# Expert slots of four, three, two and one units in a fused attention and expert kernel

## The chip, the cores and the metric

The kernel runs on one core of a Trainium2 chip. Its time is the device time of one execution in microseconds. The median of 3 runs before the change is 802.62 us (801.01 to 803.15).

## The reference

Two stages follow each other. The first is attention by feature maps: for each of 8 batches and 8 heads with 576 tokens of 64 numbers

```
phi(x) = [exp(p), exp(-p)],  p = x @ w_phi - max|x @ w_phi|      (128 features, so 256)
kv = phi(k)^T v,   z = sum over tokens of phi(k)
x = phi(q) kv / (phi(q) z + 1e-6)                                (8 heads side by side: 512 numbers)
```

The second is a layer of 8 experts over the 4608 tokens. A token takes the expert with the largest logit of `x @ w_gate`, or, if it is not the first of its batch and a local gate is at least 0.5, the expert of the token before it. Then

```
h = relu(x @ w1[e])          (512 -> 1024)
out = p[e] * (h @ w2[e])     (1024 -> 512),  p = softmax(logits)
```

So the list of tokens of each expert is known only once attention is done, and it depends on the data.

## The kernel before

**Attention** (`step`, L400) is a loop of 72 steps of two chunks of 128 tokens: projection, exponentials, sums over keys, output, and the gate's logits. The 4608 tokens come in four quarters (`bp` 0 to 3). When a quarter's logits are there, `gate` (L452) runs beside the following steps as a generator, a few small DVE operations a step: it finds each token's expert, its rank in the expert's list and its probability, and scatters the pairs (token, probability) to `lst` in DRAM with nine indirect DMAs on POOL (L571). The gate of the last quarter can only run behind attention.

**Units and slots.** A unit is 128 tokens of one expert's list. A slot is a number of units of one expert: its weights are loaded once, eight pieces of 512 KB (four of `w1`, four of `w2`, `load`, L848). A piece lands in a staging tile `wraw`, ACT rounds it to `whi` (L876), and DVE makes the residue `wlo` (L877). Each product is three matmuls, hi by hi, hi by lo and lo by hi (`three`, L941). Before the change there are quads (four units, done as two groups of two), pairs and singles; and "duals", slots that do a half unit of each of two experts at once, straight in f32 (L956).

**Layer 1** (`layer1`, L958) of a group of two units holds the weights in the array and moves the tokens: 8 blocks of hidden features by 4 blocks of inputs by 3 products, 96 matmuls with 256 moving columns. Two blocks of features share one PSUM bank (`psl`, two banks); ACT evacuates it with a relu to `hh` (L978) and DVE makes the residue `hl` (L979). A single holds the tokens and moves the weights (48 matmuls of 256 columns), which leaves the hidden layer the wrong way round: it is transposed on TensorE by 8 transposes (`turn`, L995). **Layer 2** (`layer2`, L1010) holds 128 tokens of the hidden layer and moves 512 columns of weights: 24 matmuls a unit. The result is scaled on DVE (L1030) and scattered to the output by an indirect DMA on POOL (L1033).

**Tokens** are fetched a unit at a time by an indirect DMA (L904) and turned by four transposes (L929) into `xhi` and `xlo`. `slots` (L1042) runs a list of slots; it turns the next slot's tokens within the current one (`between`, `rest`) and loads the coming slots' weights each time that a weight buffer comes free (`used`, `spare`). There are 13 weight buffers (`WE`, `WR`, `WL`: 8 + 4 + 1), of which 12 exist during the early slots.

**Early slots and the plan.** Three early pairs fill the time in which the last gate and the plan of the rest are made. `plan_early` (L666) places two of them once half of the tokens are known and one more at three quarters; their lists are fetched and turned, and the first slot's weights are loaded, still beside attention. In the first early slot's layer 1 the list `soon` runs a step of the last gate after certain blocks (`go` is one step, `rest` is all that is left, which ends with the nine scatters). `more` runs one part of `plan_main` (L727): the first part counts the units of each expert, cuts them level by level (quads, pairs, singles), makes each unit's row in the list and issues the fetch of the lists (`lr`, L633); the second turns the fetched lists on TensorE (L646) to `tok` and `prob`. The first `more` stands in the second unit of the first early slot's layer 2, the second in that of the second slot. After the early slots the memory of attention is given back (`open_rest`), and with it comes the second set of weight staging tiles.

The number of slots of each size is fixed: 3 quads, 7 pairs, 4 singles and 2 duals always run. Units that find no place run one at a time in a loop behind a condition (`guarded`, L1069); the last slot's output is written behind that condition (`held`). The order of the main slots is written out in `moe` (L1104): the quads first, then the pairs, with a single or a dual after every one or two of them. TensorE's order is the program's, but for small moves of the compiler's own planner.

## Time and profile before

| | before |
|---|---|
| median of 3 runs | 802.62 us (801.01 to 803.15) |
| the profiled execution | 799.24 us |
| its span | 797.3 us |
| granted TensorE clock, mean | 0.991 |
| TensorE busy | 771.4 us, 97% of the span |
| VectorE (DVE) busy | 511.8 us, 64% |
| ScalarE (ACT) busy | 401.6 us, 50% |
| GpSimd (POOL) busy | 159.8 us, 20% |
| HBM | 128.21 MB read, 22.06 MB written |
| attention | up to 318.2 us |
| three early slots | 318.2 to 406.3 us |
| sixteen main slots | 406.3 to 791.3 us |

All times in a row of the profile are microseconds from the span's start, a mean is in ns. A group's line has the source line, the engine, the operation, what it writes and reads with shapes, the count, then its busy time, the mean of one, and the idle time of the engine ahead of it with what ended it. TensorE's matmuls overlap in the pipeline, so that their shown durations are longer than the distance from one start to the next. "issue" is time in which an engine waited for nothing that the profile shows. Of the rows by stretch, the columns are the stretch, its length, the busy time and count of PE, PEld (weight loads), DVE, ACT and POOL, the granted TensorE clock, the DMA engines' mean busy share, and GB/s.

### The profile page before, as it was taken

What the parts mean: (1) busy time and instruction counts of PE and PEld (TensorE: products, weight loads), DVE (VectorE), ACT (ScalarE), POOL (GpSimd) and SP (SyncE); (2) the same over time, 40 slices, a digit from 0 to 9 for tenths busy, and PEclk for the clock granted to TensorE, in tenths of its full rate; (3) what the DMA queues carried; (4) which work ended last, traced back from release to release, by engine and by line L of the source; (5) the groups of instructions that cost most, each with busy time, mean ns of one, the idle gap of its engine ahead of it and who ended that gap; (6) DMA issues with size and microseconds to landing.
All of it is one profiled execution on the core that took longest, in us unless ns stands there. A gap on an engine that the chain in (4) does not pass through costs nothing.

```text
span 797.3 us, 23203 instructions
## 1 busy us (share of the span) xinstructions
PE 771.4 (97%) x9674; PEld 678.8 (85%) x9674; DVE 511.8 (64%) x939; ACT 401.6 (50%) x708; POOL 159.8 (20%) x174
## 2 busy tenths in 40 slices
PE   7999999999999999969999999999999999999997
PEld 6999989988888878958899898598999999499996
DVE  5787798789878876956654223742965941759641
ACT  4666666666687655523543022631844721748431
POOL 0200002200375132152331201211222211111010
PEclk9999999999999999988999999999999999999999
DMA  7755545444687521716942575842867749968500
GB/s 205 228 154 136 132 133 147 127 132 123 204 250 230 170 62 42 219 37 219 401 166 85 195 270 220 293 133 97 312 218 232 291 151 403 388 230 292 199 34 29
DMA packets 75595, 151.29 MB, mean 190 GB/s; under 512 B 8524, under 2 KB 48652, under 8 KB 75446
## 3 DMA queue, kind: packets, MB, share of 16 engines
q1 hardware_dynamic: 67280, 127.27, 49.4%
q0 software_dynamic: 8032, 22.45, 7.8%
q8 instruction: 77, 1.26, 0.6%
q14 instruction: 30, 0.25, 0.1%
q10 hardware_dynamic: 176, 0.07, 0.0%
HBM read 128.21 MB, written 22.06 MB: 188 GB/s over the span
## 4 chain that ended last, share of the span: by engine, by line
PE 85%; DVE 7%; issue 3%; DMA 3%; ACT 2%; POOLq 0%; SPq 0%; another core or an unknown queue 0%; POOL 0%; DVEq 0%; ACTq 0%
PE l L943 15%; PE l L944 15%; PE l L945 15%; PE kvp L269 9%; PE nm L328 9%; PE pj L227 8%; PE qt L247 4%; PE l L956 4%; DMA wraw<-in_w1h 2%; PE tr L929 2%; DVE m L230 2%; DVE sb L232 1%; PE nm L307 1%; PE nm L295 1%; ACT kp L236 1%
## 5 line engine op out<-in xcount | busy, mean ns | idle before, releaser
L876 ACT CAST whi<-wraw 128x1024 fp32r<-128x1024 f32 x136 | 142.2, 1047 | 160.2 <-PE l L945 61.9
L877 DVE TENSOR_TENSOR wlo<-wraw,whi 128x1024 fp32r<-128x1024 f32 x128 | 156.3, 1222 | 76.3 <-ACT whi L876 69.6
L943 PE MATMUL l<-xhi,whi 128*128 128x256 f32 x512 | 146.9, 287 | 2.4 <-issue 1.4
L944 PE MATMUL l<-xlo,whi 128*128 128x256 f32 x512 | 144.4, 282 | 1.3 <-issue 1.3
L945 PE MATMUL l<-xhi,wlo 128*128 128x256 f32 x512 | 144.5, 282 | 0.9 <-issue 0.9
L943 PE MATMUL l<-whi,hh 128*128 128x512 f32 x288 | 114.8, 398 | 4.7 <-DVE p_rim L621 4.1
L230 DVE TENSOR_REDUCE m<-pj 128x8 f32<-128x1024 f32 x72 | 87.8, 1219 | 46.4 <-PE pj L227 44.2
L945 PE MATMUL l<-whi,hl 128*128 128x512 f32 x288 | 113.3, 393 | 0.6 <-DVE hl L979 0.6
L944 PE MATMUL l<-wlo,hh 128*128 128x512 f32 x288 | 113.0, 392 | 0.0
L250 ACT ACTIVATE qp<-qt 128x512 f32<-128x512 f32 x144 | 84.9, 604 | 55.4 <-PE qt L247 55.1
L236 ACT ACTIVATE kp<-sb 128x512 f32<-128x512 f32 x144 | 82.8, 622 | 51.5 <-DVE sb L232 42.3
L943 PEld LDWEIGHTS l<-xhi,whi 128*128 128x128 f32 x512 | 97.6, 191 | 4.5 <-issue 2.0
L945 PEld LDWEIGHTS l<-xhi,wlo 128*128 128x128 f32 x512 | 97.6, 191 | 2.2 <-issue 2.1
L944 PEld LDWEIGHTS l<-xlo,whi 128*128 128x128 f32 x512 | 97.6, 191 | 1.4 <-issue 0.9
L232 DVE TENSOR_TENSOR sb<-pj,m 128x1024 f32<-128x1024 f32 x72 | 88.1, 1224 | 4.1
L328 PE MATMUL nm<-kvs,qp 128*64 128x74 f32 x2304 | 88.0, 228 | 1.8 <-issue 1.4
L227 PE MATMUL pj<-first,kq 64*128 64x128 f32 x1152 | 85.7, 289 | 4.1 <-DMA kq<-in_kqT 4.1
L1033 POOL DMA_INDIRECT out<-y,p_tokm x31 | 39.2, 1264 | 245.0 <-DVE y L1030 232.0
L328 PEld LDWEIGHTS nm<-kvs,qp 128*64 128x64 f32 x2304 | 79.8, 136 | 3.5 <-issue 2.6
L227 PEld LDWEIGHTS pj<-first,kq 64*128 64x128 f32 x1152 | 71.8, 191 | 9.4 <-issue 4.1
L269 PE MATMUL kvp<-v,kp 128*64 128x65 f32 x2048 | 76.7, 224 | 0.1
L978 ACT ACTIVATE hh<-l 128x512 fp32r<-128x512 f32 x64 | 38.0, 594 | 69.7 <-PE l L945 60.3
(230 smaller groups left out, 1059.3 us busy)
## 6 DMA issues: line engine op xcount, KB each, us to landing
wraw<-in_w1h SPq DMA_DIRECT2D x68, 512.0 KB
wraw<-in_w2h SPq DMA_DIRECT2D x68, 512.0 KB
kq<-in_kqT SPq DMA_DIRECT2D x47, 384.0 KB
v<-in_va SPq DMA_DIRECT2D x48, 195.0 KB
xs<-xo SPq DMA_DIRECT2D x48, 128.0 KB
whi<-in_w1h SPq DMA_DIRECT2D x8, 512.0 KB
wlo<-in_w1h SPq DMA_DIRECT2D x8, 512.0 KB
whi<-in_w2h SPq DMA_DIRECT2D x8, 512.0 KB
```

The costliest lines, as they stand in the source:

```text
L227: self.last_pe = self.pe.matmul(t[:, h, i % 2, j, :], kq[r, j, s], self.w2[r], start=True, stop=True)
L230: dve.tensor_reduce(m, f, AX.X, ALU.max, apply_absolute_value=True)
L232: self.last_dve = dve.tensor_sub(sb.rearrange("p h c j f -> p (h c j) f"), f, m.unsqueeze(2).broadcast_to([128, 8, 128]))
L236: self.last_act = act.activation(kp[:, :, :, sg, :].rearrange("p c h f -> p h c f"), sb[:, :, :, 0], AF.Exp, scale=1.0 - 2 * sg)
L250: self.act.activation(qp[:, sg], t, AF.Exp, scale=1.0 - 2 * sg)
L269: self.pe.matmul(self.kvp[r, sg, h], self.ch[i]["kp"][:, h, sg, r], self.v(i, b)[:, h], start=first and n < 2, stop=last and n >= 6)
L328: self.pe.matmul(e["t"][r, c - c0, h, :], self.ch[i]["qp"][:, sg, h, q0 + r.start:q0 + r.stop], kvs[:, sg, h, :], start=sg == 0, stop=sg == 1)
L876: self.act.copy(hi, raw)
L877: (low or self.dve).tensor_sub(lo, raw, hi.bitcast(F32))
L943: mm(o, ah, bh, start=first, stop=False)
L944: mm(o, ah, bl, start=False, stop=False)
L945: self.last_pe = mm(o, al, bh, start=False, stop=last)
```

## The change

A slot now has four, three, two or one units, and all its tokens are the moving columns of layer 1 at once: 512, 384 or 256 columns for each held block of weights, 96 matmuls in each case. With three or four units, one block of features fills a tile of PSUM; with two, two blocks do. Quads are no longer two groups. Singles keep the old form (`layer1_one`), which duals use too.

There are 2 early slots of three units, both placed at half of the tokens, in place of 3 of two; 4 quads, 4 threes, 1 pair and 2 duals in the main list, and no single outside the guarded loop, which now may run up to 14. The main order is quad and three in turn, then the pair, with the duals third and seventh. `plan_main` has one more level (units by three, by a multiplication and a shift), and a new generator `table` works out the constants of it on DVE during seven attention steps. All of the next slot's tokens are turned within layer 2 of the current slot, or within layer 1 of a single or a dual. Steps of the gate and of the plan now stand after every six matmuls or block: four gate steps in slot 0's layer 1, the first part of the plan in the third unit of slot 0's layer 2, the second in slot 1's layer 1. The tiles of `x` and of the hidden layer exist once, the second set of weight staging has two tiles for three, and one weight buffer moves from the pool that is there early to the one that comes later (8 + 3 + 2).

```diff
-WE, WR, WL = 8, 4, 1
+WE, WR, WL = 8, 3, 2
...
-HALFWAY, EARLY, QUADS, PAIRS, SINGS, GUARD, DUALS, GUARD_D = 2, 3, 3, 7, 10, 6, 4, 2
-NUE = 2 * EARLY
+EARLY, QUADS, TRIPS, PAIRS, ONES, GUARD, DUALS, GUARD_D = 2, 4, 4, 1, 14, 14, 4, 2
+SINGS = 3 * TRIPS + ONES
+SIZES = ((4, QUADS), (3, TRIPS), (2, PAIRS), (1, ONES))
+FIRST = {4: 0, 2: 4 * QUADS, 3: 4 * QUADS + 2 * PAIRS, 1: 4 * QUADS + 2 * PAIRS + 3 * TRIPS}
+NUE = 3 * EARLY
...
+                    if p == FILL + 4:
+                        self.background.append(self.table())
...
-            self.slots(self.eslots, soon=[no, self.fetched_last, go, no, go, no, go, rest], later=[[no, no, more]] * 2)
+            self.slots(self.eslots, soon=[[no, no, no, go, no, no, go, no, no, go, rest], [no, no, no, no, more]],
+                       later=[[no, no, more]])
...
+    def table(self):
+        dve = self.dve
+        t = self.const.tile([NU, 16], F32, name="table")
+        c = [t[:, i:i + 1] for i in range(16)]
+        u, (v, size, rest, q, two, one, notq) = self.tokid[0:NU, 0:1], [self.slotc[:, i:i + 1] for i in range(7)]
...
+        def by_three(o, x, n):
+            dve.tensor_scalar(o, x, 3.0, None, ALU.is_ge)
+            for k in range(2, n):
+                dve.scalar_tensor_tensor(o, x, 3.0 * k, o, ALU.is_ge, ALU.add)
+        yield STEP
+        by_three(eth, u, EARLY)
+        dve.scalar_tensor_tensor(erest, eth, -3.0, u, ALU.mult, ALU.add)
+        yield STEP
+        dve.tensor_scalar(c[11], u, 2.0, None, ALU.mult)
+        dve.tensor_scalar(c[12], u, 2.0, 1.0, ALU.mult, ALU.add)
...
+        self.eslot, self.eparts, self.duo = eth, erest, t[:, 11:13]
+        self.mslot = cq, sz, half
+        self.kinds, self.pasts = (q, three, two, real), (notq, past, real)
...
-        if bp in (1, 2):
-            self.background.append(self.plan_early(bp))
+        if bp == 1:
+            self.background.append(self.plan_early())
...
+        f = self.floats(self.thirds(self.units_so_far(0, 7, "e"), "e"), "fe")
...
+        slots = [dict(ei=[ei[3 * i:3 * i + 1]], u=3 * i, n=3, name=f"e{i}", rows=2 * TB) for i in range(EARLY)]
         self.eslots += slots
...
+        f = self.fetch(es, k, NUE, "e", WAIT)
...
+        yield from self.early_chores(slots, got())
...
+        for i, (n, cap) in enumerate(SIZES):
+            if n == 3:
+                fi = self.thirds(r, "3")
+            elif n == 1:
+                fi = r
+            else:
+                fi = self.psm([NU, E], f"fi{n}", I32)
+                dve.tensor_scalar(fi, r, n.bit_length() - 1, None, ALU.logical_shift_right)
+            f = self.floats(fi, f"f{n}")
+            ins = self.prefix(f, f"i{n}")
+            incl, cnt = mix(ins, incl, kind[i], f"im{n}"), mix(f, cnt, kind[i], f"cm{n}")
+            if n > 1:
+                pl = self.placed(f, ins, cap, f"pl{n}")
+                dve.tensor_scalar_mul(pl, pl, float(n))
+                nr = self.psm([NU, E], f"r{n}", I32)
+                dve.tensor_sub(nr, r, pl)
+                r = nr
+                bef = mix(pl, bef, past[i], f"bef{n}")
+        i1 = ins
...
-        self.mxt = self.mkpool(root, "moe_x2", 2, "right")
+        self.mxt = self.mkpool(root, "moe_x2", 1, "right")
...
-            dst = [rp.tile([128, 1024], F32, name="wraw", bufs=3)]
+            dst = [rp.tile([128, 1024], F32, name="wraw", bufs=3 if rp is self.mxg else 2)]
...
+                p = self.mxt if n > 1 else self.ml1
+                s["x"] = [p.tile([128, 4, n * 128], F32R, name=x + "1" * (n == 1)) for x in ("xhi", "xlo")]
...
-    def layer1(self, s, gi, between, soon=()):
-        pe, act, dve = self.pe, self.act, self.dve
-        xh, xl = s["x"][gi]
-        w, last = s["w"], gi == len(s["n"]) - 1
-        hp = self.ml1 if gi else self.mx2
-        hh = hp.tile([128, 8, 256], F32R, name="hh", bufs=1)
-        hl = hp.tile([128, 8, 256], F32R, name="hl", bufs=1)
-        s.setdefault("h", []).append((hh, hl))
-        if s["n"][gi] == 2:
-            for f2 in range(4):
-                t = self.psl.tile([128, 2, 256], F32, name="l1")
-                wh, wl = w[f2]
-                for j in (0, 1):
-                    for d in range(4):
-                        c = slice(d * 256 + j * 128, d * 256 + j * 128 + 128)
-                        self.three(t[:, j, :], wh[:, c], wl[:, c], xh[:, d, :], xl[:, d, :], d == 0, d == 3)
-                    if soon:
-                        soon[2 * f2 + j]()
-                hc = slice(2 * f2, 2 * f2 + 2)
-                act.activation(hh[:, hc, :], t, AF.Relu)
-                dve.scalar_tensor_tensor(hl[:, hc, :], t, 0.0, hh[:, hc, :].bitcast(F32), ALU.max, ALU.subtract)
-                if between:
-                    between.pop(0)()
-                if last:
-                    self.used(1)
-                else:
-                    self.spare()
-            return []
...
+    def hidden(self, n):
+        return [self.mx2.tile([128, 8, n * 128], F32R, name=x, bufs=1) for x in ("hh", "hl")]
+    def layer1(self, s, between):
+        act, dve = self.act, self.dve
+        (xh, xl), w, n = s["x"], s["w"], s["n"]
+        hh, hl = s["h"] = self.hidden(n)
+        def pause():
+            if between:
+                between.pop(0)()
+        per = 2 if n == 2 else 1
+        for f0 in range(0, 8, per):
+            t = self.psl.tile([128, per, n * 128], F32, name="l1")
+            for j in range(per):
+                f = f0 + j
+                wh, wl = w[f // 2]
+                for d in range(4):
+                    c = slice(d * 256 + f % 2 * 128, d * 256 + f % 2 * 128 + 128)
+                    self.three(t[:, j, :], wh[:, c], wl[:, c], xh[:, d, :], xl[:, d, :], d == 0, d == 3)
+                    if d % 2 and (d, j) != (3, per - 1):
+                        pause()
+            hc = slice(f0, f0 + per)
+            act.activation(hh[:, hc, :], t, AF.Relu)
+            dve.scalar_tensor_tensor(hl[:, hc, :], t, 0.0, hh[:, hc, :].bitcast(F32), ALU.max, ALU.subtract)
+            pause()
+            if (f0 + per) % 2 == 0:
+                self.used(1)
+    def layer1_one(self, s, between):
+        pe, act = self.pe, self.act
+        xh, xl = s["x"]
+        hh, hl = s["h"] = self.hidden(1)
+        hs = self.ml1.tile([128, 1024], F32, name="hs", bufs=1)
...
-            if between and q in (0, 2):
+            if between:
...
     def slots(self, order, held=None, soon=(), later=()):
         first = order[0]
-        for g in range(len(first["n"])):
-            for f in self.tokens(first, g):
-                f()
+        for f in self.tokens(first):
+            f()
         self.held = len(first.get("w", ()))
         self.coming = list(order)
         for i, s in enumerate(order):
             while len(s.get("w", ())) < 8:
                 self.spare()
             new = order[i + 1] if i + 1 < len(order) else None
-            last = len(s["n"]) - 1
-            for gi in range(last):
-                self.layer1(s, gi, [])
-            between = self.tokens(new, 0, bool(soon) and i == 0) if new else []
-            rest = self.layer1(s, last, between, () if i else soon)
+            between = self.tokens(new, bool(soon) and i == 0) if new else []
+            if s["n"] > 1:
+                self.layer1(s, list(soon[i]) if i < len(soon) else [])
+                rest = between
+            else:
+                rest = self.layer1_one(s, between) + between
             if i < len(later):
-                rest = list(later[i])
-            for f in between:
+                rest = rest + list(later[i])
+            self.layer2(s, rest, None if new else held)
+            for f in rest:
                 f()
-            for gi in range(last + 1):
-                self.layer2(s, gi, rest, None if new else held)
-            if new and len(new["n"]) == 2:
-                for f in self.tokens(new, 1):
-                    f()
             s.clear()
...
-        few = self.ss[:SINGS - GUARD]
+        big = [x for i in range(max(QUADS, TRIPS)) for n in (4, 3) for x in self.by_size[n][i:i + 1]]
+        order = big + self.by_size[2] + self.by_size[1][:ONES - GUARD]
         for i, x in enumerate(self.ds[:DUALS - GUARD_D]):
-            few.insert(3 * i, x)
-        rest = self.qs + self.ps_
-        order = []
-        per = len(rest) / len(few)
-        for i, x in enumerate(few):
-            order += rest[round(i * per):round((i + 1) * per)] + [x]
+            order.insert(2 + 4 * i, x)
```

166 lines of the change are left out of this document (64 added, 102 removed).

## The prediction

> **What bounds the kernel now.** I read the page's share of engines, then the busy time by stage, then the chain of waits, then single instructions in order of time.
>
> ```profile
> PE 771.4 (97%) x9674; PEld 678.8 (85%) x9674; DVE 511.8 (64%) x939; ACT 401.6 (50%) x708; POOL 159.8 (20%) x174
> ```
>
> Busy time by stage (columns: stretch, us, busy and count of PE, PEld, DVE, ACT, POOL, granted clock, DMA share, GB/s). The stretches are attention, the three early slots, the main slots, the end:
>
> ```profile
> 4.00:318.20 314.20, 307.72 (x6678) 276.16 (x6679) 250.03 (x542) 200.12 (x429) 60.54 (x80) 1.00 0.54 156
> 318.20:406.30 88.10, 78.31 (x486) 68.30 (x484) 61.55 (x167) 39.38 (x48) 29.16 (x27) 0.94 0.64 218
> 406.30:791.30 385.00, 384.99 (x2515) 334.30 (x2513) 199.38 (x229) 160.64 (x230) 67.95 (x56) 1.00 0.60 214
> 791.30:797.30 6.00, 0.36 (x2) 0.00 (x0) 0.75 (x1) 0.00 (x0) 0.98 (x1) 0.70 0.11 44
> ```
>
> TensorE sets the main stage: idle for 0.01 us of 385, with ACT and DVE about half empty. Fewer casts or weight loads buy nothing there; only a shorter TensorE stream does. The early stage is the one with idle time. Its busy time overlaps (matmuls are pipelined), so what a matmul really takes is read from starts. TensorE's instructions, first and last of a run of 120 at 256 columns and of 96 at 512:
>
> ```profile
> 516.44 0.36 PE L943 MATMUL l<-xhi,whi 128*128 128x256 f32 x1
> 530.48 0.28 PE L945 MATMUL l<-xhi,wlo 128*128 128x256 f32 x1
> ...
> 429.93 0.40 PE L943 MATMUL l<-whi,hh 128*128 128x512 f32 x1
> 451.60 0.40 PE L945 MATMUL l<-whi,hl 128*128 128x512 f32 x1
> ```
>
> (530.48 - 516.44) / 119 = 0.1180 us at 256 columns and 21.67 / 95 = 0.2281 us at 512. The shown 0.28 and 0.40 are not costs. So doubling the columns nearly doubles the time: only 2 x 0.1180 - 0.2281 = 0.008 us of a matmul is fixed. No row has 384 columns. In proportion it is 0.171 by the one row and 0.177 by the other; at worst it is as slow as 512. I take the middle of the rows, 0.1731, since both lie on nearly one line through zero.
>
> **The main stage, part by part.** Before, layer 1 there is 13 groups of two units (three quads of two groups, seven pairs) of 96 matmuls and four singles of 48, all at 256 columns: (1248 + 192) x 0.1180 = 169.9 us. After, it is 384 at 512, 384 at 384 and 96 at 256: 87.6 + 66.5 + 11.3 = 165.4. That is **-4.5**. Layer 2 stays: the same 30 units of 24 matmuls at 512.
>
> The singles go, and with them their turning of the hidden layer. One single slot:
>
> ```profile
> 561.60 0.28 PE L943 MATMUL l<-whi,xhi 128*128 128x256 f32 x1
> 565.06 0.28 PE L945 MATMUL l<-whi,xlo 128*128 128x256 f32 x1
> 565.17 0.38 PE L995 MATMUL tr<-first,hs 128*128 128x128 f32 x2
> 565.31 0.36 PE L943 MATMUL l<-whi,xhi 128*128 128x256 f32 x1
> 566.45 0.60 PE L929 MATMUL tr<-first,xg 128*128 128x128 f32 x4
> 566.80 0.36 PE L943 MATMUL l<-whi,xhi 128*128 128x256 f32 x1
> 574.54 0.28 PE L943 MATMUL l<-xhi,whi 128*128 128x256 f32 x1
> ```
>
> Two transposes cost 0.14 us, four times per single, four singles: **-2.2**. A set of four token transposes costs 0.35; there is one per unit in both kernels. Sixteen main slots become eleven; the single took 12.94 us to the next slot's start, 0.5 more than 48 x 0.1180 + 24 x 0.2281 + 4 x 0.14 + 2 x 0.35, so a switch costs up to 0.5, at least 0; I take 0.4: **-2.0**. The 40 expert weights saved (five slots) are 20 MB of loads, 40 casts and 40 differences on engines with room here: 0, covered by TensorE's own work. The sum is **-8.7**, with bounds -5 (0.177, switches free) and -10 (0.171, 0.5 a switch). At 0.2281, which the rows speak against, it would be +12, and +11 more in the early stage.
>
> The plan must fit. The counts that the reference's routing gives for its inputs leave (3 4 6 3 3 3 4 4) units per expert after two early threes; four quads, four threes and one pair take exactly these 30, so the guarded loop does not run.
>
> **The early stage.** Its TensorE work is before 3 x (96 x 0.1180 + 48 x 0.2281) = 66.8, six token sets 2.1 and some 2 for the gate's small matmuls: 71 of 88.1 us, so 17 are lost. After, 2 x (96 x 0.1731 + 72 x 0.2281) = 66.1, eight sets 2.8 and 2: again 71. What changes is the loss. TensorE, DVE and POOL in order of time, then TensorE's clock:
>
> ```profile
> 348.50 0.96 POOL L571 DMA_INDIRECT lst<-pr,ri  x1 [0.30 <-issue]
> 349.64 0.28 PE L944 MATMUL l<-xlo,whi 128*128 128x256 f32 x1 [0.83 <-issue]
> 351.07 0.17 DVE L584 TENSOR_TENSOR_SCAN p_i<-p_one,p_f 36x8 f32<-36x8 f32 x1 [1.11 <-DVE p_ohh L792]
> 354.03 0.60 ACT L978 ACTIVATE hh<-l 128x512 fp32r<-128x512 f32 x1 [9.41 <-DVE p_kh L795]
> 359.21 0.13 DVE L621 TENSOR_SCALAR p_rim<-p_rowm 36x1 int32<-36x1 f32 x1
> 359.43 0.76 PE L943 MATMUL l<-whi,hh 128*128 128x512 f32 x1 [4.12 <-DVE p_rim L621]
> 360.92 0.92 POOL L633 DMA_INDIRECT lr<-lst,p_rim  x1 [0.30 <-issue]
> ...
> 354.00:360.00 6.00, 1.88 (x8) 1.52 (x8) 6.00 (x24) 1.67 (x3) 1.33 (x2) 0.50 0.34 104
> 360.00:364.00 4.00, 4.00 (x21) 3.90 (x20) 3.14 (x4) 2.58 (x3) 1.53 (x2) 0.55 1.01 339
> ```
>
> Right behind nine list scatters in a row (338.4 to 349.5 us) all engines issue slowly until 354, with the main plan's small operations in the middle of it; then the delayed plan and weight differences stand ahead of the hidden layer on DVE, and TensorE waits to 359.4. From 347.0 on it did 24 matmuls (2.8 us) in 12.4: 9.6 lost, and about 2 more at half clock. The remaining 5 go at the end, where the first main slot's weights arrive late. The chain of waits shows it (start, us, what):
>
> ```profile
> 339.75 0.16 PE pt L655 x2
> 375.25 0.35 PE pt L646 x2
> 375.72 0.33 SPq L866
> 377.42 8.32 DMA wraw<-in_w1h
> ```
>
> In the changed kernel the scatters stay where they are (the gate's steps come after 24, 42, 60 and 66 matmuls at 0.1731: 4.2 to 11.4 us, as before). DVE was slow from 343.4 on, TensorE only from 348.5: it had 5 us issued ahead. Now it works on 512-column matmuls there, which last about twice as long, so 2 to 3 us of the 10.5 are left; I take 2.7 lost (bounds 0 and 9.6). The plan's first step moves to the third unit of slot 0's layer 2: 318.2 + 0.4 + 16.6 + 0.9, then 57 matmuls at 0.2281 and 1.8 for token sets and small matmuls, is 351, with 2.7 is 353.7: behind the slow stretch. Its second step (the list's transposes, which TensorE waits for in order, layer 1 of slot 1 queued behind) moves to 30 matmuls into slot 1: 353.7 + 3.4 + 5.2 = 362.3. Before, 35.5 us lay between the two; now 8.6. In them DVE does some 85 plan operations by the code (76 before). Here a new wait is made. DVE at its free pace:
>
> ```profile
> 340.36 0.16 DVE L732 TENSOR_TENSOR p_r<-p_um,p_tkf 36x8 int32<-36x8 int32 x1
> 343.24 0.20 DVE L753 SCALAR_TENSOR_TENSOR p_cm<-p_f,consts,p_cm 36x8 f32<-36x8 f32 x1
> ```
>
> 33 in 2.9 us: 7.4 for 85, some 2.5 for evacuations between; then 0.92 to issue the fetch and 0 to 5.8 for its data (0.36 MB by the 0.5 MB load that took 8.32 in a full queue); I take 2.5, since slot 1's loads are done by then. The list is there at 367, TensorE waits **4 to 5**, and 1.5 more at low clock. What follows on SP and POOL (the main slots' register loads, first weights and four gathers) starts at 367, not 376, and has 30 us: nothing lost; without that cover it is the 5 us of before. So 71 + 2.7 + 4.5 + 1.5 = 79.5, **-8.6** (bounds -17 and +6).
>
> By the Trainium skill ("TensorE: Matmul & The Clock Gate", section "What's actually happening") the clock halves only after an idle window of about 3.4 us, so a shorter wait would spare the 1.5; by it the median would be 784.
>
> **Attention.** The table's 16 small DVE operations of about 0.16 us are spread over seven steps with DVE idle a fifth of the time; the second early plan's 22 go with its fetch. Without cover either is 2.5 to 3.5 us; together I take 0 (bounds -3 and +3). Two more early gathers on POOL, 80% idle, are free; the two that stood at 322 go. The third token set ahead of slot 0 is counted above. The fewer copies of x, h and weight staging tiles cost 0, since TensorE's order puts the last reader ahead of the next writer; if not, an evacuation (0.594 + 0.686) for each of 13 slots, 17. Weight buffers in the early stage fall from 12 to 11: slot 1's eighth weight loads in slot 0's last unit, 25 us ahead of its use, free too.
>
> **Sum.** The profiled execution took 799.24 us (span 797.3 and 1.9 around it), 3.4 below the median 802.62. -8.7 - 8.6 - 0 = -17.3: 782 for such an execution, **785** for the median.
>
> By the Trainium skill (same page, section "Wait — 56ns, not 53.3ns?") a warm matmul costs N / 2.4 GHz plus about 2.5 ns. The rows show 8 ns fixed, so the trace disagrees in size; by the page's figure 576 fewer main matmuls save 1.4 and not 4.5, and the median would be 788.
>
> **Rivals.** *No new wait:* the plan is done in time and nothing starves: 71 + 2, 6.5 more saved, **779**. For it: only 5 us of overlap are missing. Against: TensorE is in order.
>
> *The plan stays slow:* if it again takes the 27 us from 339.75 to the list's landing (360.92 + 0.92 + up to 5.8), the list comes at 380.7, TensorE waits 18.4 and 2.3 at low clock: early 94.4, +6.3, and **800**. For it: other scatter traffic could slow it again. Against: the scatters end ahead of it.
>
> *The columns bring nothing:* if the 8 ns are no fixed cost but lie in where the two runs stand, the 4.5 fall away: **790**. For it: two short runs carry the 8 ns. Against: other such runs look alike. The Trainium skill's figure above comes near this case.
>
> *Slower: evacuation bounds layer 1 of the threes.* A tile there is 12 matmuls, 2.08 us, with two banks.
>
> ```profile
> L877 DVE TENSOR_TENSOR wlo<-wraw,whi 128x1024 fp32r<-128x1024 f32 x128 | 156.3, 1222 | 76.3 <-ACT whi L876 69.6
> L876 ACT CAST whi<-wraw 128x1024 fp32r<-128x1024 f32 x136 | 142.2, 1047 | 160.2 <-PE l L945 61.9
> L978 ACT ACTIVATE hh<-l 128x512 fp32r<-128x512 f32 x64 | 38.0, 594 | 69.7 <-PE l L945 60.3
> L979 DVE SCALAR_TENSOR_TENSOR hl<-l,hh 128x512 fp32r<-128x512 f32 x64 | 43.9, 686 | 43.5 <-ACT hh L978 42.5 <-issue 1.0
> ```
>
> If cast and difference get ahead of relu and residue (three quarters of 0.594 and 0.686), one tile takes 1.05 + 0.45 + 1.22 + 0.51 = 3.2 against 2.08: 1.1 lost on every second of 48 tiles, 27 us, **812**. It decides from some 16 of the 24 on. Against: the same order before would have lost 0.7 per tile of 2.83, and the main stage shows 0.01 idle.
>
> *It does not do what it says:* a unit left over runs in the guarded loop, 13 us and its loads: **810**; the counts speak against it.
>
> **Numbers.** Forecast 0.55, no new wait 0.17, plan slow 0.10, columns nothing 0.10, evacuation 0.06, guarded loop 0.02. The first, second and fourth are faster, and 0.04 of the third; a measurement of this kernel tells about 0.3% (2.4 us) from no change. Faster 0.86, same 0.06, slower 0.08. The range holds the bounds of the early stage and the plan rival nearly: 774 to 798.
>
> **What would show it.** Right: 384-column starts near 0.173 us apart; main stage near 376 us, TensorE never idle; early stage near 80 with a wait at the list's transposes in slot 1. Wrong: idle ahead of L943 in layer 1 of threes, a guarded slot at the end, an early stage over 90, or attention longer than 321.

## The result and the profile after

The changed kernel took **794.02 us** (median of 4 runs, 793.57 to 794.46) against 801.82 (4 runs, 800.82 to 803.15) for the kernel before: a ratio of **0.9902, 95% interval 0.9883 to 0.9920**, 7.8 us faster where 17.3 were forecast. The profiled execution took 793.57 us with a span of 791.8; that of before had 799.24 and 797.3, so the two traces differ by 5.5 us of span.

The share of engines and then busy time by stage of the changed kernel (attention, two early slots, main slots, end; columns as before):

```profile
PE 768.5 (97%) x8967; PEld 652.2 (82%) x8967; DVE 459.6 (58%) x896; ACT 351.4 (44%) x648; POOL 152.0 (19%) x175
```

```profile
4.00:320.99 316.99, 309.19 (x6682) 277.98 (x6682) 252.34 (x541) 202.55 (x432) 61.96 (x83) 1.00 0.56 159
320.99:402.53 81.54, 75.97 (x387) 65.31 (x387) 50.84 (x166) 27.89 (x40) 29.31 (x28) 0.98 0.43 152
402.53:785.90 383.37, 383.19 (x1901) 308.92 (x1899) 155.60 (x188) 119.46 (x174) 58.55 (x53) 1.00 0.45 163
785.90:791.80 5.90, 0.18 (x1) 0.00 (x0) 0.75 (x1) 0.00 (x0) 0.98 (x1) 0.95 0.12 46
```

| stage | before | after | measured | forecast |
|---|---|---|---|---|
| attention (from 4.00) | 314.20 | 316.99 | +2.8 | 0 (-3 to +3) |
| early slots | 88.10 | 81.54 | -6.6 | -8.6 |
| main slots | 385.00 | 383.37 | **-1.6** | **-8.7** |
| end | 6.00 | 5.90 | -0.1 | 0 |

DVE's and ACT's work in the main stage fell by a fifth and more (199.38 to 155.60 and 160.64 to 119.46 us), POOL's by 9, and no time came of it: TensorE stayed busy for 383.19 of 383.37 us. So the gain went missing in TensorE's own stream.

**The main stage, product by product.** From the start of every TensorE instruction to the next start, summed over the main stage (working from all rows of the trace; the stage's sum is 384.9 before, 383.2 after, to the last product's start):

| what | before | after | difference | forecast |
|---|---|---|---|---|
| layer 1 of quads, threes, pairs, singles | 172.85 (1440 products) | 169.87 (864) | -3.0 | -4.5 |
| layer 2 of the same | 166.19 (719) | 169.04 (719) | **+2.9** | 0 |
| turning the hidden layer | 5.12 | 2.94 | -2.2 | -2.2 |
| turning tokens | 11.11 | 11.20 | +0.1 | 0 |
| duals | 29.67 | 30.12 | +0.4 | 0 |
| slot switches, five fewer | in the rows above | | | -2.0 |

**Several cadences.** A cadence is here the steady distance from one product's start to the next. TensorE in order of time, first and last of stretches that nothing interrupts: before at 256 columns (102 steps, then 48, then 24), after at 384 (72 steps), at 512 in layer 1 (60) and at 512 in layer 2 (33).

```profile
407.85 0.28 PE L943 MATMUL l<-xhi,whi 128*128 128x256 f32 x1
419.86 0.28 PE L943 MATMUL l<-xhi,whi 128*128 128x256 f32 x1
...
458.40 0.28 PE L943 MATMUL l<-xhi,whi 128*128 128x256 f32 x1
464.16 0.28 PE L943 MATMUL l<-xhi,whi 128*128 128x256 f32 x1
...
524.32 0.28 PE L943 MATMUL l<-xhi,whi 128*128 128x256 f32 x1
527.04 0.28 PE L943 MATMUL l<-xhi,whi 128*128 128x256 f32 x1
```

```profile
450.32 0.34 PE L954 MATMUL l<-xhi,whi 128*128 128x384 f32 x1
463.04 0.34 PE L954 MATMUL l<-xhi,whi 128*128 128x384 f32 x1
...
584.86 0.39 PE L954 MATMUL l<-xhi,whi 128*128 128x512 f32 x1
598.86 0.39 PE L954 MATMUL l<-xhi,whi 128*128 128x512 f32 x1
...
751.26 0.39 PE L954 MATMUL l<-whi,hh 128*128 128x512 f32 x1
758.74 0.39 PE L954 MATMUL l<-whi,hh 128*128 128x512 f32 x1
```

At 256 columns that is 0.1178 us in the first stretch, 0.1200 in the second and 0.1133 in the third, all of the same kernel; at 512 it is 0.2333 and 0.2267; at 384 it is 0.1767 here. The fastest goes by the columns alone (2 x 0.1133 = 0.2267): there is no fixed cost per product in it. The slowest adds 0.0067 us to a product of 256 or of 512.

The two rows on which the forecast rested hold several cadences each. The run of 256 columns from 516.44 is 0.1200 for some 70 products and 0.1133 for some 50, and the run of 512 from 429.93 is 0.2289 in its first half and 0.2267 in the rest. Above all, the second row stands in layer 2, while layer 1 of the changed kernel runs at 0.2333 for the most part. The 8 ns between twice the first row and the second are no fixed cost.

Had all layer-1 products kept the fastest cadence, layer 1 would take 163.2 us in both kernels, since 1440 x 256 and 384 x 512 + 384 x 384 + 96 x 256 are the same columns. If each step is counted with at most 0.0067 above the fastest, the slower cadences add 6.7 us before and 4.6 after: some 2 of layer 1's -3.0. The rest of it and layer 2's +2.9 are waits: the first product behind a transpose is some 0.09 us late, the token sets moved from layer 1 to layer 2, and the singles' turnings are gone (2.8 us less in layer 1, 1.6 more in layer 2, 20 places for 39).

**Waits at layer 1's banks.** All engines in order of time, changed kernel:

```profile
407.46 0.68 DVE L994 SCALAR_TENSOR_TENSOR hl<-l,hh 128x512 fp32r<-128x512 f32 x1
407.89 0.40 PE L956 MATMUL l<-xhi,wlo 128*128 128x512 f32 x1
408.19 0.19 PEld L954 LDWEIGHTS l<-xhi,whi 128*128 128x128 f32 x1 [0.34 <-DVE hl L994]
...
554.07 0.39 PE L954 MATMUL l<-whi,hh 128*128 128x512 f32 x1
554.52 0.39 PE L956 MATMUL l<-whi,hl 128*128 128x512 f32 x1
554.89 0.42 PE L954 MATMUL l<-xhi,whi 128*128 128x384 f32 x1
```

At 408.19 a product waits for the residue to leave one of the two banks. At 554.07 the program's own scheduler, foreseeing such a wait, has set layer-2 products between two tiles of layer 1; the switch back takes 0.37 us for a product of 0.23. Such places, 31 in all, cost 3.2 us after the change against 0.9 before (11 places). That is +2.3 where the five fewer switches were to bring -2.0.

**Early stage and attention.** TensorE and DVE in order of time, changed kernel, and last a row by stretch:

```profile
319.66 0.66 PE L940 MATMUL tr<-first,xg 128*128 128x128 f32 x4
320.99 0.44 PE L954 MATMUL l<-xhi,whi 128*128 128x384 f32 x1 [0.68 <-ACT xhi L949]
...
356.52 0.21 PE L697 MATMUL pt<-cnt,consts 128*44 128x8 bf16 x2
370.67 0.15 DVE L663 TENSOR_SCALAR p_rim<-p_rowm 44x1 int32<-44x1 f32 x1
376.10 0.31 PE L688 MATMUL pt<-first,lr 48*128 48x48 f32 x1
393.44 1.23 DVE L887 TENSOR_TENSOR wlo<-wraw,whi 128x1024 fp32r<-128x1024 f32 x1 [1.48 <-issue]
394.59 0.74 DVE L1045 TENSOR_SCALAR y<-l,p_probe 128x512 f32<-128x512 f32 x1
395.39 0.79 PE L954 MATMUL l<-whi,hh 128*128 128x512 f32 x1 [2.39 <-DVE y L1045]
...
395.39:399.00 3.61, 3.61 (x9) 2.89 (x10) 2.72 (x4) 2.99 (x5) 2.09 (x3) 0.54 1.05 415
```

Layer 1 of the first early slot waits for the third token set (320.99). The plan runs from 356.52 to 370.67, the list's transposes follow at 376.10 without a wait worth a name, and TensorE waits at 395.39 for a scaling on DVE that stands behind the weight difference of 393.44. Behind this wait of 2.39 us the granted clock is 0.54 on average from 395.39 to 399.00, and a product lasts twice as long.

One thing must be known to read the runs below: they fell under **two conditions** that the kernel does not set. In the result above and in the second to fourth group of experiments the kernel before took 799.7 to 801.8 us; in the first and the last group 787.3 to 787.5. The record names the same chip number for the first and the second group, so the number does not tell the conditions apart. From here on the first condition is the one of the result, in which the kernel before takes about 800 us. Each kernel is set beside the kernel before of its own group.

### The profile page after: what moved, and what is told of

It is laid out like the page before. It is cut to its first block, busy times and chain, and to the rows that moved or that the text cites. A ratio compares the mean times of both kernels' runs of the same rounds, so it can differ in the third digit from the quotient of the medians.

```text
span 791.8 us, 21376 instructions
## 1 busy us (share of the span) xinstructions
PE 768.5 (97%) x8967; PEld 652.2 (82%) x8967; DVE 459.6 (58%) x896; ACT 351.4 (44%) x648; POOL 152.0 (19%) x175
## 5 line engine op out<-in xcount | busy, mean ns | idle before, releaser
L886 ACT CAST whi<-wraw 128x1024 fp32r<-128x1024 f32 x88 | 92.2, 1048 | 141.8 <-PE l L956 63.8
L887 DVE TENSOR_TENSOR wlo<-wraw,whi 128x1024 fp32r<-128x1024 f32 x80 | 97.6, 1223 | 86.3 <-ACT whi L886 83.7
L954 PE MATMUL l<-xhi,whi 128*128 128x384 f32 (+2 forms) x352 | 126.2, 359 | 0.9 <-ACT xhi L949 0.7
L955 PE MATMUL l<-xlo,whi 128*128 128x384 f32 (+2 forms) x352 | 124.2, 353 | 0.1
L956 PE MATMUL l<-xhi,wlo 128*128 128x384 f32 (+2 forms) x352 | 124.3, 353 | 0.0
L993 ACT ACTIVATE hh<-l 128x384 fp32r<-128x384 f32 (+1 forms) x84 | 44.9, 535 | 133.6 <-PE l L956 129.3
L994 DVE SCALAR_TENSOR_TENSOR hl<-l,hh 128x384 fp32r<-128x384 f32 (+1 forms) x84 | 51.4, 612 | 61.2 <-ACT hh L993 61.0
L954 PEld LDWEIGHTS l<-xhi,whi 128*128 128x128 f32 x352 | 66.0, 188 | 15.4 <-issue 5.1
L311 PEld LDWEIGHTS kvp<-v,kp 128*64 128x64 f32 x2048 | 67.6, 139 | 5.9 <-issue 5.5
L955 PEld LDWEIGHTS l<-xlo,whi 128*128 128x128 f32 x352 | 66.1, 188 | 6.0 <-DVE xlo L950 0.4
```

Of the source, the lines that this page charges most:

```text
L311: self.pe.matmul(self.kvp[r, sg, h], self.ch[i]["kp"][:, h, sg, r], self.v(i, b)[:, h], start=first and n < 2, stop=last and n >= 6)
L886: self.act.copy(hi, raw)
L887: (low or self.dve).tensor_sub(lo, raw, hi.bitcast(F32))
L954: mm(o, ah, bh, start=first, stop=False)
L955: mm(o, ah, bl, start=False, stop=False)
L956: self.last_pe = mm(o, al, bh, start=False, stop=last)
```

## The experiments

**1. The width alone.** Layer 1's tile of one feature block is filled in two halves of the columns; nothing else changes. In `e1_split` all slots of three and four units, in `e15_quads` only the four-unit ones:

```diff
+                half = 256 if n == 2 else n * 64        # e1_split: 256 and 192 columns
+                half = 384 if n == 3 else 256           # e15_quads: 256, threes stay at 384
+                for g in range(0, n * 128, half):
+                    x = slice(g, g + half)
...
-                    self.three(t[:, j, :], wh[:, c], wl[:, c], xh[:, d, :], xl[:, d, :], d == 0, d == 3)
+                        self.three(t[:, j, x], wh[:, c], wl[:, c], xh[:, d, x], xl[:, d, x], d == 0, d == 3)
```

> Undoes the width alone: each 512- or 384-column product of layer 1 becomes two of 256 or 192, everything else of the changed kernel stays. Theory P (time is proportional to the columns; the 8 ns a matmul of the prediction were two mixes of a fast and a slow cadence, 113 and 120 ns at 256, 227 and 233 at 512): starts of 0.118 at 256 and 0.085 to 0.092 at 192; 768 x 0.1182 - 384 x 0.2329 = +1.3 and 768 x 0.090 - 384 x 0.1753 = +1.8, so the main stage is about 386 us, +3, and the time 797 against 794. Theory F (8 ns fixed per matmul, gain eaten by waits for the layer-1 banks): +0.008 x 768 = +6.1 us in the main stage, and the waits at the banks unchanged: 800. If 192 columns are bounded by the weight load, above 0.1 a start, +8 or more: neither.

> Only the four-unit slots' layer 1 is split, into two times 256 columns; threes, pair and both early slots stay. Theory P (256 columns cost half of 512, in either of the two cadences 113 and 120, 227 and 233): 768 x 0.1177 - 384 x 0.2333 = +0.8, main stage within 1.5 us of the changed kernel's, time +0 to +1.5. Theory F (8 ns fixed per matmul, as predicted): +3.1 from 384 more of them, time +3.

`e15_quads`: 795.83 us, ratio 0.9944 (0.9928 to 0.9961), beside 794.44 and 0.9930 (0.9905 to 0.9954) for the changed kernel in its group. By stretch, its main stage, and TensorE in the 192-column stretch of `e1_split` (81 steps):

```profile
400.77:785.00 384.23, 383.84 (x2284) 326.65 (x2282) 155.43 (x188) 119.48 (x174) 59.63 (x54) 1.00 0.46 163
```

```profile
478.77 0.27 PE L954 MATMUL l<-xhi,whi 128*128 128x192 f32 x1
487.81 0.27 PE L954 MATMUL l<-xhi,whi 128*128 128x192 f32 x1
```

Four profiles of the changed kernel have main stages of 382.7 to 385.0 us to the last product's start, `e15_quads` 383.9. The quads' layer 1 took 117.1 ns a product at 256 columns (763 recorded, 89.35 us; 89.9 for 768) and 235.2 at 512 (384, 90.33 us). Theory P holds: twice as many products of half the width cost the same, and the fixed 8 ns do not exist. The time above the fastest cadence does not go by the number of products either: counted as above it is 4.4 us in layer 1 of `e15_quads`, with 384 products more, and 4.6 in the changed kernel. `e1_split` shows where width does matter: a product of 192 columns takes 0.1116 us and not 0.085. That is a floor, just under the 0.1133 of 256 columns. The threes' layer 1 so cost 89.2 us instead of 68.1, the main stage 404.0; its early stage took 118 us at a granted clock of 0.87, with waits of up to 9 us, and says nothing of the width. In all 841.5 us in the profiled execution, ratio 1.0679 (1.0632 to 1.0727): both theories had missed the floor, and only the remark on it was near.

The Trainium skill ("TensorE: Matmul & The Clock Gate", section "LDWEIGHTS (loading the stationary operand)") has a load of P columns of weights take P / 1.2 ns, an estimate of 107 ns for the 128 here. Its section "Back-to-back issue gap" says that load and product together set the spacing. By that the floor would be the weight load, and the 0.1116 is within 5 ns of it; no run here changed the load, so that the cause of the floor is not shown.

**2. A third bank for layer 1**, taken from the transposes:

```diff
-        self.psl = self.mkpool(root, "moe_ps2", 2, "right", PSUM)
+        self.psl = self.mkpool(root, "moe_ps2", 3, "right", PSUM)
-        if hasattr(self, "psr") and self.trn % 3:
-            return self.psr.tile([128, 4, 128], F32, name="tr")
+        if hasattr(self, "psr") and self.trn % 2:
+            return self.psr.tile([128, 4, 128], F32, name="tr", bufs=1)
```

> A third PSUM bank for layer 1's tiles, taken from the transposes (two left in the main stage). The changed kernel's main stage has layer-2 products set between the tiles of layer 1 and extra time at these places: 0.67 + 0.74 us behind them, 1.20 ahead of them, 0.40 inside, 3.0 in all. Theory B (the two one-bank tiles with their evacuation make the order and the waits): these go, main stage 380.4 against 383.4 us, time 791. Theory N (the places cost as much as any change of weights and form, whatever the banks): 0, time 794; slower by up to 2 if the transposes now wait for their banks.

> e2_banks again, the third bank alone. Main stage 381 us against 383 to 385 of the changed kernel; the early stage 79 us as in e2_banks against 81 to 82. Where the kernel before takes 800 us: ratio 0.985 to 0.988 if both carry over, 0.988 to 0.990 if only the main stage does.

784.12 us, ratio 0.9959 (0.9941 to 0.9977); again 784.16, 0.9961 (0.9948 to 0.9974). Both groups had the other condition, so the changed kernel's measure there is `e5_list` (below), 789.76 and 1.0029.

```profile
394.60:775.85 381.25, 381.25 (x1905) 311.12 (x1903) 157.28 (x190) 120.36 (x175) 62.71 (x54) 1.00 0.46 166
```

Theory B holds. TensorE is never idle, layer-2 products no longer stand between layer 1's tiles, and of the 3.2 us at such places 0.4 are left; layer 2 falls by 1.5 us, layer 1 by 1.2, and the duals' second layer, now short of a bank, gives back 0.95. The main stage is 381.0 us to the last product's start in both runs. That is less than half of the 5.6 us gained: the early stages are shorter too, 79.1 and 78.7 us against 81.95 in `e5_list`, and what the third bank does there was not followed up.

**3. The plan back in its old place**, at the start of slot 0's second layer, right behind the nine list scatters; and the list's transposes asked for earlier:

```diff
-                       later=[[no, no, more]])        # e4_plan1, e4_again
+                       later=[[more]])
-                rest = rest + list(later[i])
+                rest = list(later[i]) + rest
...
-            self.slots(self.eslots, soon=[[...], [no, no, no, no, more]],        # e5_list
+            self.slots(self.eslots, soon=[[...], [more]],
```

> Puts the main plan's first step back to the beginning of slot 0's second layer, right behind the last list scatters are issued, as near to them as before the change; all else stays. Theory S (the prediction: the plan's DVE work inside the slow spell is what cost the kernel before its 9.6 us): the spell of 343 to 348 us starves TensorE again, 5 to 10 us lost there, though the list comes some 8 us earlier and the main slots' first weights with it (6.5 us lost at the end of the early stage in the changed kernel shrink to 1): 794 to 798. Theory L (the spell needs nothing of the plan; what counts is when the list comes): nothing lost at the spell beyond the 1.9 us of the changed kernel, the early stage about 5 us shorter, 789.

> Asks for the list's transposes at the first place of slot 1's layer 1 rather than at the fifth; the plan's first step stays. The prediction had TensorE wait 4 to 5 us at these transposes, in order; the trace shows them behind 86 products of that layer and no wait. Theory O (the order written by the program is what TensorE runs): the transposes stand behind some 6 to 12 products, at 361 us, the list lands about 375, so 10 us or more of wait, little of it won back: 797 or more. Theory R (the program's scheduler sets them where it reckons that the list is there, whatever place asks for them): the same order within 2 us, no wait, 794.

`e4_plan1` took 790.08 us, ratio 1.0042 (1.0026 to 1.0058); `e5_list` 789.76, 1.0029 (1.0014 to 1.0044). `e5_list` came out with the same instructions in the same order on every engine as the changed kernel, two tiles of layer 1 with other numbers: theory R, the transposes are set where the program's scheduler reckons the list to be there. So it serves as a run of the changed kernel under the other condition, and there **the change does not gain, it loses 0.3%**. The runs of both kernels in three more groups, and `e4_plan1` once more, were to show whether that comes from the spell at the list scatters (theory D) or from a chip that is faster as a whole (theory G).

> The kernel before, unchanged, for a second profile: in the first experiments the kernel before took 787.5 us on the chip they ran on, and not 801.8. Theory G (chips differ as a whole): all stages are shorter in the same measure, the early stage 86 to 88 us with TensorE starved for some 10 us at 347 to 359, the main stage 383 or more. Theory D (the spell behind the list scatters is what differs): attention and the main stage within 5 us of the first profile, the early stage under 82 us, and the spell costs TensorE under 4 us.

> The changed kernel, unchanged, on the same chip as the kernel before of this job. Theory G: ratio 0.990 again, whatever the chip. Theory D: the 8 us were the spell of the kernel before on the first chip; where that kernel takes some 787 us the ratio is 0.998 to 1.004; where it takes 802 it is 0.990.

> The kernel before again, for a profile under this job's conditions. In the first experiments the kernel before took 787.5 us, in the second 800.2, the changed kernel 793.4 in the second; step 66 of attention (behind three list scatters in a row) lasted 6.9 us in the second and 4.2 in the first. Theory D (the slow issue behind list scatters changes from job to job): if that step is 4.2 here, the kernel before is near 787 and its early stage near 80 us, with under 4 us lost at 347 to 361; if it is 6.9, it is near 800 and the early stage 88. Theory G (all is slower alike) has the early stage at 88 in both.

> The changed kernel in the same job. Theory D: ratio 0.998 to 1.004 if the kernel before takes about 787 us here, 0.990 to 0.993 if it takes about 800. Theory G: 0.990 to 0.993 in both.

> The kernel with the plan's first step back at the beginning of slot 0's second layer, as in e4_plan1. Theory S (plan work inside the spell costs TensorE): where the kernel before takes about 800 us, 5 to 9 us lost at 341 to 350 and the time 3 to 6 above the changed kernel; where it takes about 787, as in e4_plan1, 3 to 4 lost and the time within 1 of the changed kernel. Theory L (only the list's time counts): 0 to 2 below the changed kernel in both.

> The kernel before, for its profile in this job. Theory D: where step 66 of attention lasts 4.2 us, the early stage is 80 us or less and the time near 787; where it lasts 6.9 us, 88 and 800.

> The changed kernel in the same job. Theory D: early stage 81 to 82 us in either case; ratio 1.000 to 1.004 where step 66 lasts 4.2 us, 0.990 to 0.993 where it lasts 6.9.

All three groups had the first condition: before 800.17, 799.72 and 800.40, the changed kernel 793.36, 792.66 and 794.44, ratios 0.9917 (0.9903 to 0.9932), 0.9905 (0.9882 to 0.9929) and 0.9930 (0.9905 to 0.9954). Since none fell under the other condition, they cannot tell D from G by themselves; it is the ratio 1.0029 of `e5_list` and the rows below that speak for D. `e4_again` took **800.87**, 1.0011 (0.9994 to 1.0028): with the plan alone put back the whole gain is gone. Its early stage, beside that of before in the same group (`b_third`) and of `e5_list`:

```profile
321.80:409.98 88.18, 78.44 (x386) 66.96 (x387) 52.41 (x168) 29.60 (x42) 30.52 (x28) 0.94 0.47 158
```

```profile
318.51:406.71 88.20, 77.98 (x488) 68.43 (x485) 61.84 (x167) 39.53 (x48) 29.34 (x27) 0.94 0.63 218
```

```profile
316.73:398.68 81.95, 76.05 (x386) 65.32 (x387) 50.82 (x166) 27.88 (x40) 29.06 (x28) 0.98 0.43 152
```

The same plan operations of the same program, DVE in order of time under the other condition (`e4_plan1`) and under the first (`e4_again`):

```profile
331.54 0.23 DVE L699 TENSOR_SCALAR p_um<-pt 44x8 int32<-44x8 f32 x2 [0.20 <-PE pt L697]
336.95 0.21 DVE L755 SCALAR_TENSOR_TENSOR p_bef<-p_pl,table,p_bef 44x8 f32<-44x8 f32 x1
342.09 0.13 DVE L812 TENSOR_SCALAR p_over<-p_i 1x1 f32<-1x1 f32 x1
```

```profile
337.35 0.23 DVE L699 TENSOR_SCALAR p_um<-pt 44x8 int32<-44x8 f32 x2 [0.20 <-PE pt L697]
344.60 0.22 DVE L755 SCALAR_TENSOR_TENSOR p_bef<-p_pl,table,p_bef 44x8 f32<-44x8 f32 x1
353.78 0.13 DVE L812 TENSOR_SCALAR p_over<-p_i 1x1 f32<-1x1 f32 x1
```

10.6 us become 16.4. Theory S holds under the first condition (a spell of slow issue, and what is queued in it is late), and most of it is absent under the other. The spell also shows in attention. The step within which three list scatters are issued, in the kernel before under the first condition and in `e5_list` under the other:

```profile
276.26 1.16 PE L227 MATMUL pj<-first,kq 64*128 64x128 f32 x16
283.11 1.16 PE L227 MATMUL pj<-first,kq 64*128 64x128 f32 x16
```

```profile
276.15 1.16 PE L269 MATMUL pj<-first,kq 64*128 64x128 f32 x16
280.30 1.16 PE L269 MATMUL pj<-first,kq 64*128 64x128 f32 x16
```

6.85 us against 4.15; all fourteen profiles of the first condition have 6.75 to 7.44 there, all six of the other 4.15. No profile of the kernel before fell under the other condition, so that its early stage is some 9 us shorter there is worked out only: 13 us less in all, some 4 of them in attention, as in the changed kernel.

The traces tell the conditions apart in one more way. All six of the other condition hold landing times for POOL's indirect DMAs (58 to 102 of 116), and none of the fourteen of the first holds one. The packets themselves are not slower: around the plan those of the scatters' queue took 25 ns in the mean in `e4_again` and 26 in `e4_plan1`. So the conditions may come from the machine or its settings; the cause stays open.

**4. Scatters further apart**, with the plan in its old place: first by POOL fills between them, then by tying each to the landing of the one before:

```diff
+            for _ in range(10):                          # e13_spaced, ahead of each scatter
+                ins = self.pool.memset(t, 0.0).ins
...
+                at = self.small.tile([128, 1], I32, name="at", bufs=1)     # e16_apart
+                pool.tensor_copy(at, ri[:, c:c + 1])
```

> The plan's first step at the beginning of slot 0's second layer as in e4_plan1, and ten small POOL fills (about 0.2 us each) ahead of each of the nine list scatters, so that they come some 3 us apart and not 1.26. The list then comes as late as in the changed kernel or later. Theory Z (scatters in close succession slow the issue of all engines): the plan's operations run 0.07 to 0.2 us apart instead of 0.7, TensorE loses under 2 us at 340 to 360, the time is within 3 of the changed kernel. Theory Y (the spell comes with the plan's own small operations, or with something else at this place): 8 us lost there again, and the list still late: 4 to 10 above the changed kernel.

> As e4_plan1 (the plan's first step at the beginning of slot 0's second layer), with the nine list scatters of the last gate each waiting for the landing of the one before, so that they come 3 us or more apart instead of 1.26. Theory Z (scatters in close succession slow the issue of all engines): the plan's operations run at 0.07 to 0.2 us instead of 0.7, TensorE loses under 3 us at 340 to 360; the list comes at about 370 as in the changed kernel, the time is within 3 of it (0.990 to 0.995 where the kernel before takes 800). Theory Y (not the closeness of the scatters): 6 us or more lost there again, 1.000 or more.

Neither decided it. In `e13_spaced` (801.67 us, 1.0014, 0.9993 to 1.0036) the scheduler set all fills ahead of the first scatter, so that it is a second `e4_again`, early stage 91.3. In `e16_apart` (793.61, 1.0078, 1.0055 to 1.0102) the scatters came some 3 us apart, but under the other condition, where there was hardly a spell to remove; the list came 5.6 us later than in `e4_plan1`, early stage 85.9. Whether the spell needs scatters in close succession stays open.

**5. Late weights and the third token set.** `e8_pool` gives the first main slot's eight weight differences to POOL, `e7_third` turns the third token set of the first early slot into a bank of layer 1; `e11_all` joins the third bank, the third set, and POOL for the four differences of layer 2 only.

```diff
+        order[0]["low"] = self.pool                     # e8_pool; e11_all for four of eight
-        (low or self.dve).tensor_sub(lo, raw, hi.bitcast(F32))
+        (low or s.get("low") or self.dve).tensor_sub(lo, raw, hi.bitcast(F32))
+        if self.trn == 3:                               # e7_third
+            return self.psl.tile([128, 4, 128], F32, name="l1")
```

> The eight weight differences of the first main slot go from DVE to POOL (2.38 us each there, 1.22 on DVE). At the end of the early stage TensorE loses about 6.5 us, the most of it (2.7 us) where a layer-2 bank waits for its scaling on DVE, which stands behind a difference whose weights have not landed. Theory Q (in-order DVE is what makes the late weights cost): 2.5 to 4 of it go, early stage 78 to 79 us, time 3 less than the changed kernel. Theory R (the weights themselves, or ACT's casts, are late): no gain, and POOL's longer differences delay the first product of the main stage: 0 to +3.

> The third token set of the first early slot is turned into a bank of layer 1's pool, idle at that time, instead of waiting for the bank of the first set. Between the last step of attention and the first product of layer 1 lay 15.9 us after the change, 13.8 before. Theory T (the third set waits for its bank, and layer 1 of all 384 columns for the third set): 14 to 14.5 us, time 1.5 less than the changed kernel. Theory U (the set is late because its gather is, or the order there has another cause): 15.9, no difference.

> The third bank for layer 1, the third token set in a bank of its own, and POOL for four of the first main slot's differences (those of the second layer, needed 20 us later; with all eight TensorE waited 9.5 us for POOL). By the single runs -2.3 in the main stage, -2.2 at attention's end, -3 in the early stage if DVE's order makes that loss; where two of them overlap less. Theory Q (in-order DVE): 5 to 7 below the changed kernel. Theory R (POOL again late for the second layer, or the loss only moves): 2 to 4 below.

`e8_pool`: 801.63, ratio 1.0024 (1.0011 to 1.0038). By stretch (early, main), then in order of time:

```profile
319.49:398.06 78.57, 73.93 (x382) 63.65 (x382) 38.45 (x155) 25.02 (x38) 35.42 (x29) 1.00 0.36 124
398.06:793.60 395.54, 385.97 (x1904) 311.03 (x1904) 163.22 (x192) 122.53 (x177) 71.51 (x61) 0.99 0.46 165
```

```profile
402.98 5.95 DVE L887 TENSOR_TENSOR wlo<-wraw,whi 128x1024 fp32r<-128x1024 f32 x1 [4.14 <-ACT whi L886]
403.14 4.70 POOL L887 TENSOR_TENSOR wlo<-wraw,whi 128x1024 fp32r<-128x1024 f32 x2
412.92 0.68 DVE L994 SCALAR_TENSOR_TENSOR hl<-l,hh 128x512 fp32r<-128x512 f32 x1
413.66 0.80 PE L954 MATMUL l<-xhi,whi 128*128 128x512 f32 x1 [9.13 <-DVE hl L994]
```

The early stage is 3.6 us shorter than in the changed kernel of its group (82.19), as theory Q has it: in-order DVE made that loss. But while POOL worked on two differences, DVE's next one took 5.95 us instead of 1.22, the residue behind it came at 412.92, behind a relu on ACT that was itself late (411.45), and TensorE waited 9 us for its bank. The sum is worse. `e7_third`: 791.63, 0.9914 (0.9885 to 0.9942), not told apart from the 0.9917 of its group by its time; in the trace layer 1 runs steadily from 14.7 us behind the last attention step instead of 15.9, theory T, and from that step to the last product it is 478.6 us against 480.8. `e11_all`: 790.09, **0.9865 (0.9844 to 0.9887)** beside the changed kernel's 0.9905: 2.6 us faster than the changed kernel, not 5 to 7; the two intervals just touch (0.9882 is the lower end of the other). The main stage is 381.0; from the last attention step to it nothing was gained (97.4 against 96.8), so theory R for that part.

## Why the prediction came out wrong

**The step that failed** is the main stage's layer 1: "only 2 x 0.1180 - 0.2281 = 0.008 us of a matmul is fixed". The first row stands in layer 1 and the second in layer 2, and each holds several cadences. In layer 1 of the changed kernel the 512-column products run at 0.2333 in a steady stretch and cost 0.2352 in the mean, twice the 0.1171 of the 256-column products that `e15_quads` put in the same place. So the fixed cost is zero within what these runs tell, and the width brought nothing that can be measured. The term of -4.5 measured -3.0: some 2 of it because fewer of the stretches fell into a slower cadence, which no run ties to the width, and the rest from waits that moved to layer 2. There they belong to the +2.9 of a term that was put at 0. The rival *the columns bring nothing* was right in kind, with 0.10.

**The slots.** The -2.0 for five fewer switches does not show in the sum. A switch was costed from one single slot; the change instead moved the waits to layer 1's banks, as in the rival *evacuation bounds layer 1 of the threes*, whose place was right and whose price (27 us) was ten times too high: +2.3, and in `e2_banks`, with a third bank, the main stage gets 2.1 back. Moving the token sets and dropping the singles' turnings gave -1.2, the duals took 0.4.

**Right:** the hidden layer's transposes, -2.2 as measured; casts, loads and differences saved for nothing; TensorE never idle; the plan fits and the guarded loop does not run.

**The early stage: near in sum, wrong in parts.** 81.5 us against 79.5 forecast. Moving the plan out of the spell was the right cause, as `e4_again` shows. But the wait of 4 to 5 us at the list's transposes never came, since TensorE's order there is the scheduler's and not the program text's; the plan took 14 us and not 9.9, the duals' operations going first; so the list came at 376 and not 367, the first main weights were as late as before, and "nothing lost" at the end became about 6 us. Two errors of like size cancelled, so that the near sum is luck in part. What the prediction could not see is that this gain hangs on the condition.

**Attention** had +2.8, within its bounds but for a reason not named. By the last step it is 0.7 behind; the other 2.1 is the third token set, which was "counted above" at 0.35 and in truth holds up all of layer 1.

**The clock.** In the prediction the Trainium skill's rule ("TensorE: Matmul & The Clock Gate", section "What's actually happening") spares a wait shorter than about 3.4 us the low clock, and by it the median would have been 784. The wait that it was applied to did not come. But behind the wait of 2.39 us at 395.39 the clock was down all the same (0.54 to 399.00, some 1.7 us lost), so that this trace disagrees with the rule as it was used.

## What to carry to other kernels

A cadence is to be read from several stretches of one form in one place before two forms are compared: here one form had cadences up to 6% apart, and the difference between a row of layer 1 and one of layer 2 passed for a fixed cost. In this kernel a wider moving operand paid from 192 to 256 columns, where a floor of 0.11 us holds; from 256 to 512 the time went by the column, and a third bank for the results was worth more than the width. A gain that comes from moving work out of a disturbed stretch should be measured again at another time: here it was 0.7 to 1.0% under one condition and -0.3% under the other.

## What the runs showed of the hardware

- **Several cadences of the same product.** 0.1133, 0.1178 and 0.1200 us at 256 columns, 0.2267, 0.2289 and 0.2333 at 512, each steady for tens of products, at a granted clock of 1.00. What sets them is open; what they add to the fastest costs the changed kernel some 7 us in the main stage.
- **A spell of slow issue that comes and goes between groups of runs.** At list scatters in a row the engines issue late: the same program's plan takes 16.4 or 10.6 us, the same attention step 6.85 or 4.15, the whole kernel before 800 or 787. Whether the scatters make it is open.
- **A wait of 2.39 us was followed by about half the clock:** 0.54 granted from 395.39 to 399.00 us in the changed kernel.
- **192 columns cost as much as 256:** 0.1116 us against 0.1133.
- **A DVE difference beside POOL differences took 5.95 us**, the 4.70 of POOL's two and its own 1.22 one after the other. The Trainium skill ("SBUF — State Buffer", section "🔬 SBUF: two separate sides") has the two engines share a pair of ports under an exclusive lock, which DVE needs for an operation with two inputs from SBUF when POOL reads SBUF too. The row agrees in that the two did not share; by the trace's starts, which are rough for POOL, DVE came first by 0.16 us and yet waited.
